# Transposes of three late steps moved from TensorE to the DMA queue, and two leftover steps placed one step later

## The chip, the cores and the metric

The kernel runs on one core of one Trainium2 chip. The metric is the time in device microseconds of one execution. It is given as the median of several runs, and beside it stands one profiled execution, whose trace gives the durations used here. The engines are called as in the profile: PE (TensorE matmul), PEld (its weight load), DVE (VectorE), ACT (ScalarE), POOL (GpSimd) and SP (SyncE, which here only issues DMAs).

## What is computed

Eight batches, eight heads, 576 positions, head size 64. A retention layer (causal attention with a decay per head and no softmax) is followed by a gated unit whose gate is a causal convolution of five taps.

```python
scores = scale * np.matmul(q, k.transpose(0, 1, 3, 2))
gamma = 1.0 - 2.0 ** (-5.0 - np.arange(H, dtype=np.float32))
Dmat = np.where(rel >= 0, gamma[:, None, None] ** rel[None, :, :], 0.0)
x = np.matmul(scores * Dmat, v)          # then heads side by side: (8, 576, 512)
...
for k in range(5):
    gate_pre += conv_w[k][None, None, :] * xp[:, k:k + S, :]
gate = 1.0 / (1.0 + np.exp(-gate_pre))
out = gate * (x @ w_val) @ w_out
```

## The kernel before

**Steps.** The batches are worked in four pairs, numbered u = 0 to 3, with bb = 0 or 1 for the batch in the pair. The 576 positions of a batch are cut into two chunks of 256 (n = 0, 1) and 64 leftover positions. A *full step* treats one chunk of one batch, all eight heads. A *leftover step* treats the 64 leftover positions of both batches of a pair at once. That makes 16 full steps and 4 leftover steps, numbered 0 to 19. `REMD` says how many places after its pair's last full step a leftover step is put into the list. With `[2, 0, 2, 0]` the leftover steps are 6, 9, 16 and 19. Step 17 is the first chunk of the last batch, step 18 its second chunk, step 19 the last leftover step.

**One step.** `load` (L90 to L107) issues the DMAs of k, q and v on the SP queue: three of 512 KB for a full step, six of 128 KB for a leftover step. `cast` (L223) multiplies k and q by the decay factors on POOL and turns k, q and v into bf16 tiles `kb`, `qb`, `vb` (L236, L243). `transp` (L246) transposes `kb` and `qb` on PE against an identity, eight 128x128 blocks each for a full step and four for a leftover step (L256), and copies the results out of PSUM to `kt` on ACT and `qt` on DVE (L264, L266 in the helper `copy`). `state` and `state_sum` (L307, L325, L327) carry the sum over earlier chunks forward. `scores` (L283) multiplies `kt` and `qt`, DVE puts the mask on (L290, tile `am`), `inter` (L345) adds the part of earlier chunks, `values` (L358) multiplies by `vb`, and `evac` copies the result to the tile `xt` of the pair, or `xr` for leftovers.

**Blocks of the gated unit.** When the result of a batch is complete, `push_block` puts its work into a list: two convolutions (`conv`, L442, gate on ACT at L448), four value products (`val`, L537, with the product by the gate on DVE at L539, tile `zt`) and output products (`outp`, L544, copied by ACT at L547 to `ob` and stored by SP at L575). For a block near the end (number 8) half of the convolution runs as taps on ACT, POOL and DVE (L462 to L468), and for the last three blocks as products and taps (L478 to L502).

**What sets the order.** The schedule is written out by hand: instructions go to each engine in the program's order. Lists of short codes (`FULL`, `PART`, `LASTS`) give the order inside a step; a number such as `4.45` calls `fill`, which takes block work from the list until its cost is used up. In step s the loads of step s + 4 are issued first, then the casts of step s + 2; the transposes of step s + 1 come at the code `T`. After step 19 the codes of `TAIL` give the rest, where `w` takes the next item of the list. The SP queue holds loads and stores in one order; each DMA there uses one of eight semaphores in turn and is issued after the DMA eight places before it has landed.

Of the kernel before, what the change touches and what calls it, by code (L numbers as in the profile page):

```python
# [15 lines left out]
BF16 = mybir.dt.bfloat16  # L16
# [15 lines left out]
def kernel(  # L32
# [10 lines left out]
    nc = tc.nc  # L43
# [3 lines left out]
    P = 128  # L47
# [4 lines left out]
    HP = H // 2  # L52
# [7 lines left out]
    TPS, DSS, CAP = False, False, 2.0  # L60
    PB, EV, TE = [4, 2, 2], "DA", "AD"
    C1, LO = "PPP", "1vo23"
    PATH, TAIL, LASTS = {9: {2: 'D', 3: 'A'}, 11: {2: 'D', 3: 'A'}, 10: {0: 'D', 1: 'A', 2: 'D', 3: 'A'}}, ['w', 'w', 't9.201234', 'w', 'p10.301234', 's10.30', 't10.001234', 's10.31', 'w', 'w', 'w', 'w', 'c9.0', 't10.201234', 'w', 'p11.301', 'w', 'p11.323', 'w', 'p11.34', 's11.30', 'w', 's11.31', 'c11.0', 'v9.0', 'v9.1', 'v9.2', 'v9.3', 't11.201234', 'o9.0', 'o9.1', 'v11.0', 'v11.1', 'v11.2', 'v11.3', 'o11.0', 'o11.1', 'v10.0', 'v10.1', 'v10.2', 'v10.3', 'z10'], [['Sa', '4.5', 'I', 'Sb', 'Q5', 'G5', 'T', '7.15', 'Vb', 'p9.301234', 'Va', 's9.30', 's9.31', 'E', 'B'], ['1.8', 'I', 'Sr', 'p10.101234', '6.65', 'Vr', 's10.10', 'E', 'B', 's10.11']]
    SPL, REMD = 0, [2, 0, 2, 0]
    VC = "P"
    PULL = [2, 3]
    LATE = True
# [4 lines left out]
    at = ctx.enter_context(tc.tile_pool(name="at", bufs=3))  # L72
# [19 lines left out]
    NS = len(steps)  # L92
    st = {}

    def load(s):
        u, bb, n = steps[s]
        r = st.setdefault(s, {})
        R = 1 if bb is None else 2
        for nm, src in (("kf", k), ("qf", q), ("vf", v)):
            t = ld.tile([P, H, R, D], F32, tag=f"{nm}{R}", name=nm, bufs=2 if bb is None else 4)  # L100
            if bb is None:
                for x in range(2):
                    nc.sync.dma_start(out=t[x * HF:(x + 1) * HF, :, 0, :],
                                      in_=src[2 * u + x, :, NSC * SC:S, :].rearrange("h p d -> p h d"))
            elif s > 0:
                nc.sync.dma_start(
                    out=t.rearrange("p h r d -> p h (r d)"),  # L107
                    in_=src[2 * u + bb, :, n * SC:(n + 1) * SC, :].rearrange("h (p r) d -> p h (r d)", r=R))
            r[nm] = t
        if s == 0:  # L110

            for hv in range(2):
                hs = slice(hv * HP, (hv + 1) * HP)
                for nm, src in (("kf", k), ("qf", q), ("vf", v)):
                    nc.sync.dma_start(
                        out=r[nm][:, hs].rearrange("p h r d -> p h (r d)"),
                        in_=src[0, hs, 0:SC, :].rearrange("h (p r) d -> p h (r d)", r=2))
# [105 lines left out]
    def cast(s):  # L223
        u, bb, n = steps[s]
        r = st[s]
        R = 1 if bb is None else 2
        shp = [P, R, H, D]
        f0 = n * 2
        nb = 2 if bb is None else 4
        kb = cs.tile(shp, BF16, tag=f"kb{R}", name="kb", bufs=nb)  # L230
        qb = cs.tile(shp, BF16, tag=f"qb{R}", name="qb", bufs=nb)
        vb = cs.tile(shp, BF16, tag=f"vb{R}", name="vb", bufs=nb)

        how = C1 if s == 1 else "PP" + VC[s % len(VC)]
        for e, dst, src, f in ((how[0], kb, r["kf"], fk), (how[1], qb, r["qf"], fq)):
            (nc.vector if e == "D" else nc.gpsimd).tensor_tensor(  # L236
                dst, src.rearrange("p h r d -> p r h d"),
                f[:, f0:f0 + R, :].unsqueeze(3).to_broadcast(shp), op=ALU.mult)
        vsrc = r["vf"].rearrange("p h r d -> p r h d")
        if how[2] == "A":  # L240
            nc.scalar.copy(vb, vsrc)
        else:
            nc.gpsimd.tensor_copy(vb, vsrc)  # L243
        r.update(qb=qb, kb=kb, vb=vb)

    def transp(s, which="kq"):  # L246
        if s >= NS:
            return
        r = st[s]
        R = 1 if steps[s][1] is None else 2  # L250
        for nm in which:
            src = r[nm + "b"]
            tp = (scp if TPS else glp).tile([P, HP, R, P], BF16, tag="sc" if TPS else "gps", name="tp" + nm)
            for hp in range(HP):
                for rr in range(R):
                    nc.tensor.transpose(tp[:, hp, rr, :],  # L256
                                        src[:, rr, 2 * hp:2 * hp + 2, :].rearrange("p a d -> p (a d)"), ident)
            t = at.tile([P, HP, R, P], BF16, tag=f"{nm}t{R}", name=nm + "t", bufs=1 + R)
            copy(TE[nm == "q"], t, tp)
            r[nm + "t"] = t  # L260

    def copy(engine, dst, src):
        if engine == "A":
            nc.scalar.copy(dst, src)  # L264
        else:
            nc.vector.tensor_copy(dst, src)  # L266
# [121 lines left out]
    work = []  # L388
# [285 lines left out]
    def explicit(op):  # L674

        if op == "w":
            f, a, cost = work.pop(0)
            f(a)
            return
        b, _, a = op[1:].partition(".")  # L680
        f = blocks[int(b)][op[0]]
        if op[0] == "z":
            f()
        elif op[0] in "pt":
            f(int(a[0]), [int(x) for x in a[1:]])
        elif op[0] == "s":
            f(int(a[0]), int(a[1]))
        else:
            f(int(a))

    LOOK = 4
# [29 lines left out]
    for s in range(NS):  # L721
        u, bb, n = steps[s]
        last = u == B // 2 - 1
        if s + LOOK < NS:
            load(s + LOOK)
        if s > 1 and s + 2 < NS:
            cast(s + 2)
        for op in (PART if bb is None else FIRST if s == 0 else SECOND if s == 1 else FULL[n]) if s < NS - len(LASTS) \
                else LASTS[s - NS]:
            if op[0] in "cvopstgz":  # L730
                explicit(op)
            elif op[:2] in ("D0", "D2"):
                prep_diag(int(op[1]), nc.vector if op[3] == "D" else nc.gpsimd)
            elif s == 0 and ":" in op:

                first(op[0], "ab".index(op[1]), op[3:])
                if op[:2] == "Eb":
                    usable.append("conv2")
            elif op == "Sa":
                scores(s, GA)  # L740
            elif op == "Sb":
                scores(s, GB)
            elif op == "Sr":
                scores(s, ALL)
            elif op == "I":
                inter(s)
            elif op == "T":
                transp(s + 1)
            elif op in ("Tk", "Tq"):
                transp(s + 1, op[1])  # L750
            elif op == "C1":
                cast(1)
            elif op == "C2":
                cast(2)
            elif op[0] == "Q":
                pull(3, int(op[1]))
            elif op[0] == "G":
                pull(2, int(op[1]))
            elif op == "C3":
                cast(3)  # L760
            elif op == "WV":
                prep_wval()
                usable.append("val")
            elif op == "WO":
                prep_wout()
                usable.append("outp")
            elif op == "Va":
                values(s, GA)
            elif op == "Vb":
                values(s, GB)  # L770
            elif op == "Vr":
                values(s, ALL)
            elif op == "X":
                state(s + 1)
            elif op == "XS":
                state_sum(s + 1, 0)
                state_sum(s + 1, 1)
            elif op == "E":
                evac(s)
            elif op == "B":  # L780
                b = 2 * u + (bb or 0)
                if bb is None:
                    if u % 2 == 1:
                        push_block(xrs[u // 2], None, 0, [(b - 2 + j, NSC * SC, REM) for j in range(4)])
                elif (last and bb == 1) or b <= SPL:
                    push_block(xts[u], bb, n * SC, [(b, n * SC, SC)])
                elif n == NSC - 1:
                    push_block(xts[u], bb, 0, [(b, 0, NSC * SC)])
            else:
                fill(float(op))  # L790
    tail[0] = 0
    work.extend(late)
    for op in TAIL:
        explicit(op)
    assert not work and not any(pend.values())


# [28 lines left out]
```

## Time and profile before

| | us |
|---|---|
| median of 5 runs | 182.36 |
| lowest, highest | 181.17, 183.59 |
| the profiled execution | 183.08 |
| its span in the trace | 181.0 |

| engine | busy us | share of the span |
|---|---|---|
| PE | 156.5 | 86% |
| DVE | 125.3 | 69% |
| POOL | 109.5 | 61% |
| ACT | 105.2 | 58% |

The span is the time from the first to the last instruction in the trace; the execution's own time is 2.1 us longer. The page cuts the span into 40 equal slices of about 4.5 us and gives the busy share of each in tenths. The chain that ended last is followed back from the last instruction: at each step to what released it, or to the instruction before it on its engine. In a group's row the numbers after the bar are busy time, mean duration in ns, and the idle time of the engine before these instructions with what ended it. In rows of the timeline or the chain the first number is the start in us from the span's start, the second the duration. The granted TensorE clock is full in all slices.

### The profile page before, as it was taken

The numbers are of one execution on the slowest core, as the hardware profiler recorded it, in microseconds if no ns is written. First come the engines' busy times: TensorE is split into PE (matmuls) and PEld (weight loads), VectorE is DVE, ScalarE is ACT, GpSimd is POOL, SyncE is SP. The second block draws the span as 40 slices with busy tenths as digits, with TensorE's granted clock in tenths as the row PEclk, the third lists the DMA queues.
The fourth block names the chain that finished last, engine by engine and source line by source line (L and its number), as shares of the span: only waits on it lengthen the run. The fifth ranks groups of instructions, "written<-read, shape, count | busy, mean of one in ns | idle before, by whom it ended". The sixth has DMA issues, their size and how long they took to land.

```text
span 181.0 us, 7614 instructions
## 1 busy us (share of the span) xinstructions
PE 156.5 (86%) x3289; PEld 104.7 (58%) x3313; DVE 125.3 (69%) x240; ACT 105.2 (58%) x216; POOL 109.5 (61%) x105
## 2 busy tenths in 40 slices
PE   0479779967999998899999999698999889999991
PEld 0347557746666666566676587375669534447560
DVE  2968673569669645967479759646859897964931
ACT  6653775545561756257347655533678958689451
POOL 5059389977547957298836992497414697274300
PEclk9999999999999999999999999999999999999999
DMA  5999999999899989999998999997533003205334
GB/s 153 292 295 380 308 266 279 298 295 263 247 287 283 197 223 344 323 272 298 331 297 224 302 207 307 257 299 201 123 118 123 0 0 120 116 4 231 116 81 156
DMA packets 69183, 40.35 MB, mean 223 GB/s; under 512 B 14218, under 2 KB 63646, under 8 KB 69150
## 3 DMA queue, kind: packets, MB, share of 16 engines
q1 hardware_dynamic: 69120, 39.85, 78.5%
q8 instruction: 26, 0.43, 1.0%
q14 instruction: 7, 0.06, 0.1%
q10 hardware_dynamic: 30, 0.01, 0.0%
HBM read 30.42 MB, written 9.44 MB: 220 GB/s over the span
## 4 chain that ended last, share of the span: by engine, by line
PE 68%; DVE 13%; ACT 8%; issue 4%; DMA 3%; SPq 1%; DVEq 0%; ACTq 0%
PE ops L544 16%; PE cps L442 16%; PE vps L537 12%; DVE am L290 5%; PE o L358 4%; PE tpk L256 4%; PE sc L283 4%; PE tpq L256 4%; ACT gt L448 3%; DMA vf<-in_v_dram 3%; DVE accs L468 3%; PE o L345 3%; PE ds L307 2%; DVE sn L325 2%; DVE zt L539 2%
## 5 line engine op out<-in xcount | busy, mean ns | idle before, releaser
L236 POOL TENSOR_TENSOR kb<-kf,fk 128x1024 bf16<-128x1024 f32 (+1 forms) x19 | 32.7, 1723 | 35.9 <-DMA kf<-in_k_dram 35.8
L290 DVE TENSOR_TENSOR am<-sc,mask_c 128x512 bf16<-128x512 f32 x64 | 40.9, 681 | 4.1 <-PE sc L283 4.1
L442 PE MATMUL cps<-xt,diag 64*64 64x512 bf16 (+1 forms) x640 | 35.5, 353 | 3.0 <-issue 1.6
L236 POOL TENSOR_TENSOR qb<-qf,fq 128x1024 bf16<-128x1024 f32 (+1 forms) x19 | 32.7, 1723 | 1.6 <-DMA qf<-in_q_dram 1.0
L544 PE MATMUL ops<-wout,zt 128*128 128x512 bf16 x122 | 31.7, 380 | 1.4 <-issue 0.3
L442 PEld LDWEIGHTS <-diag 64*64 64x64 bf16 x760 | 25.3, 109 | 12.8 <-issue 4.9
L539 DVE TENSOR_TENSOR zt<-gt,vps 128x256 bf16<-128x256 f32 (+1 forms) x48 | 25.0, 549 | 9.8 <-PE vps L537 5.3
L537 PE MATMUL vps<-xt,wval 128*128 128x512 bf16 (+1 forms) x150 | 29.8, 334 | 1.9 <-ACT xt L264 0.9
L448 ACT ACTIVATE gt<-cps 128x512 f32<-128x512 f32 (+1 forms) x38 | 17.2, 505 | 22.2 <-PE cps L442 22.2
L537 PEld LDWEIGHTS <-wval 128*128 128x128 bf16 x192 | 17.7, 97 | 13.7 <-issue 1.9
L547 ACT COPY ob<-ops 128x512 f32<-128x512 f32 x34 | 19.6, 584 | 9.6 <-PE ops L544 7.4
L264 ACT COPY kt<-tpk 128x1024 bf16<-128x1024 bf16 (+1 forms) x19 | 17.5, 923 | 9.1 <-PE tpk L256 8.9
L243 POOL CAST vb<-vf 128x1024 bf16<-128x1024 f32 (+1 forms) x19 | 18.0, 948 | 5.1 <-DMA vf<-in_v_dram 4.4
L264 ACT CAST xt<-o 128x512 bf16<-128x512 f32 (+1 forms) x17 | 12.3, 722 | 14.4 <-PE o L358 11.7
L544 PEld LDWEIGHTS <-zt 128*128 128x128 bf16 x136 | 12.0, 98 | 14.5 <-DVE zt L539 2.3
L283 PE MATMUL sc<-qt,kt 64*64 64x128 bf16 (+1 forms) x576 | 18.4, 221 | 0.8 <-DVE am L290 0.8
L266 DVE CAST xt<-o 128x512 bf16<-128x512 f32 (+1 forms) x17 | 12.2, 717 | 9.5 <-PE sc L283 5.9
L327 ACT CAST w<-sn 128x256 bf16<-128x256 f32 x30 | 12.0, 405 | 9.7 <-DVE sn L323 6.0
L266 DVE COPY qt<-tpq 128x1024 bf16<-128x1024 bf16 (+1 forms) x19 | 11.9, 627 | 6.6 <-PE tpq L256 6.5
L325 DVE TENSOR_TENSOR sn<-ds,sn 128x256 f32<-128x256 f32 x23 | 9.8, 425 | 9.6 <-PE ds L307 6.3
L358 PEld LDWEIGHTS <-vb 64*64 64x64 bf16 x544 | 10.0, 106 | 7.9 <-issue 7.4
L358 PE MATMUL o<-am,vb 64*64 64x128 bf16 (+1 forms) x544 | 12.4, 216 | 2.3 <-DVE am L290 2.2
(90 smaller groups left out, 197.3 us busy)
## 6 DMA issues: line engine op xcount, KB each, us to landing
out_dram<-ob SPq DMA_DIRECT2D x31, 256.0 KB, 4.3
kf<-in_k_dram SPq DMA_DIRECT2D x15, 512.0 KB, 6.9
qf<-in_q_dram SPq DMA_DIRECT2D x15, 512.0 KB, 7.5
vf<-in_v_dram SPq DMA_DIRECT2D x15, 512.0 KB, 7.6
out_dram<-ob SPq DMA_DIRECT2D x10, 128.0 KB, 2.8
wvf<-in_moe_w_val_dram SPq DMA_DIRECT2D x2, 512.0 KB, 6.9
wof<-in_moe_w_out_dram SPq DMA_DIRECT2D x2, 512.0 KB, 7.9
kf<-in_k_dram SPq DMA_DIRECT2D x8, 128.0 KB, 5.0
```

Of the source, the lines that this page charges most:

```text
L236: (nc.vector if e == "D" else nc.gpsimd).tensor_tensor(dst, src.rearrange("p h r d -> p r h d"), f[:, f0:f0 + R, :].unsqueeze(3).to_broadc ...
L264: nc.scalar.copy(dst, src)
L266: nc.vector.tensor_copy(dst, src)
L283: nc.tensor.matmul(sc[hh][HS[x], a, rj, :].rearrange("p (r i) -> p r i", r=R), lhsT=r["kt"][HS[hh], hp, rj, HS[x]], rhs=r["qt"][HS[hh], hp ...
L290: nc.vector.tensor_tensor(am, sc[hh], mk.rearrange("p j i x -> p j (i x)").unsqueeze(1).to_broadcast(shp), op=ALU.mult)
L358: nc.tensor.matmul(o[x][HS[hh], hp, :], lhsT=r["vb"][HS[x], rj, 2 * hp + hh, :], rhs=r[("am", hps[0], hh)][HS[x], a, rj, :], start=(a == 0 ...
L442: nc.tensor.matmul(fold(cps[i][HS[r ^ i]]), lhsT=diag[HS[r], p2, kk, d0 + i, :], rhs=win(d0 + i, kk)[HS[r]], start=(kk == 0 and p2 == 0), ...
L448: nc.scalar.activation(gt, cps[i], AF.Sigmoid)
L537: nc.tensor.matmul(fold(vp), lhsT=wval[:, do, d, :], rhs=win(do, PAD), start=(do == 0), stop=(do == DT - 1))
L539: nc.vector.tensor_tensor(z[0][:, d, 0:N], g[d], vp, op=ALU.mult)
L544: nc.tensor.matmul(op, lhsT=z[0][:, d, m * P:(m + 1) * P], rhs=wout[:, d, :], start=(d == 0), stop=(d == DT - 1))
L547: nc.scalar.copy(ob, op)
```

## The change

Two settings and the code for them:

- `DTS = [17, 18, 19]`: for these three steps `transp` does nothing. Instead `cast` issues, right after the three casts, two DMA transposes on the SP queue, from `kb` to `kt` and from `qb` to `qt` (256 KB each for steps 17 and 18, 128 KB each for step 19). A DMA transpose waits on SP for the cast that writes its source. In the steps where this happens (15, 16 and 17) the loads of step s + 4 are issued after these casts and transposes instead of ahead of them. Only step 15 has such loads: those of step 19.
- `REMD = [3, 1, 2, 0]`: the leftover steps of the first two pairs become steps 7 and 10 instead of 6 and 9. The list is then: step 6 first chunk of batch 3, step 7 leftovers of pair 0, step 8 second chunk of batch 3, step 9 first chunk of batch 4, step 10 leftovers of pair 1; from step 11 on nothing moves.
- The tail's `w` codes are evened out with the number of items left in the list, so that another order still ends with an empty list.

On each engine, the order of instructions differs from before in steps 5 to 10 and by the instructions removed in steps 16 to 18; the SP queue also has the six transposes. In that queue the order from the last four stores ahead of step 19's loads is: two transposes of step 17, six loads of step 19, two transposes of step 18, two stores, two transposes of step 19, then the remaining stores.

```diff
+    DTS = [17, 18, 19]
...
-    SPL, REMD = 0, [2, 0, 2, 0]
+    SPL, REMD = 0, [3, 1, 2, 0]
...
         r.update(qb=qb, kb=kb, vb=vb)
+        if s in DTS:
+
+            for nm in ("k", "q"):
+                t = at.tile([P, R, HP, P], BF16, tag=f"{nm}t{R}", name=nm + "t", bufs=1 + R)
+                nc.sync.dma_start_transpose(out=t.rearrange("p r a i -> p (r a) i"),
+                                            in_=r[nm + "b"].rearrange("p r h d -> p (r h d)"))
+                r[nm + "t"] = t.rearrange("p r a i -> p a r i")
 
     def transp(s, which="kq"):
-        if s >= NS:
+        if s >= NS or s in DTS:
             return
...
-            f, a, cost = work.pop(0)
-            f(a)
+            if work:
+                f, a, cost = work.pop(0)
+                f(a)
...
-        if s + LOOK < NS:
+        if s + LOOK < NS and s + 2 not in DTS:
             load(s + LOOK)
         if s > 1 and s + 2 < NS:
             cast(s + 2)
+        if s + LOOK < NS and s + 2 in DTS:
+            load(s + LOOK)
...
-    for op in TAIL:
-        explicit(op)
+
+    ahead = TAIL.count("w") - len(work)
+    for op in ["w"] * -ahead + TAIL:
+        if op == "w" and ahead > 0:
+            ahead -= 1
+        else:
+            explicit(op)
```

## The prediction

> **What bounds the kernel now.** I read the page first: the busy tenths of the engines and of the DMA, and the chain that ended last.
>
> ```profile
> PE   0479779967999998899999999698999889999991
> ...
> DMA  5999999999899989999998999997533003205334
> ...
> PE 68%; DVE 13%; ACT 8%; issue 4%; DMA 3%; SPq 1%; DVEq 0%; ACTq 0%
> ...
> L264 ACT COPY kt<-tpk 128x1024 bf16<-128x1024 bf16 (+1 forms) x19 | 17.5, 923 | 9.1 <-PE tpk L256 8.9
> ...
> L266 DVE COPY qt<-tpq 128x1024 bf16<-128x1024 bf16 (+1 forms) x19 | 11.9, 627 | 6.6 <-PE tpq L256 6.5
> ```
>
> PE carries 68% of the chain and is nearly full in most slices. The DMA engines are full until about slice 28 (127 us), yet hold 3% of the chain: loads run ahead of PE. After 127 us they are almost idle. The last two rows are the evacuations that follow each transpose pair (L256): 923 ns on ACT, 627 ns on DVE.
>
> Next, the chain of waits between 124 and 152 us, where the three steps lie whose transposes go.
>
> ```profile
> 128.68 0.45 PE tpk L256 x8
> 129.12 0.45 PE tpq L256 x8
> ...
> 132.15 0.23 PE sc L283 x16
> 132.37 0.55 PE tpk L256 x8
> 132.93 0.45 PE tpq L256 x8
> 133.37 0.22 PE ops L544
> ...
> 135.54 0.42 DVE sn L325
> ...
> 146.70 0.09 DVE qt L266
> 146.78 0.17 issue
> 146.95 1.27 DVE zt L539 x2
> ```
>
> Two transpose pairs, those for steps 17 and 18, stand on the chain: PE does nothing else there. From 135.5 us DVE leads (sums, masks L290, conv taps L468). The third pair, for step 19, ran on PE at 142.96 us while DVE led; only its copy `qt` shows on the chain, 0.09 us and 0.17 us of issue.
>
> Then the SP queue, POOL, and one PE row, from the timeline.
>
> ```profile
> 118.67 4.74 SPq L575 DMA_DIRECT2D out_dram<-ob  x4
> 123.46 1.37 SPq L103 DMA_DIRECT2D kf<-in_k_dram  x2
> ...
> 126.90 1.32 SPq L103 DMA_DIRECT2D vf<-in_v_dram  x2
> ```
> ```profile
> 117.34 1.90 POOL L236 TENSOR_TENSOR qb<-qf,fq 128x1024 bf16<-128x1024 f32 x1
> ...
> 122.41 1.90 POOL L236 TENSOR_TENSOR qb<-qf,fq 128x1024 bf16<-128x1024 f32 x1
> ```
> ```profile
> 138.36 0.22 PE L283 MATMUL sc<-qt,kt 64*64 64x128 bf16 x1
> ```
>
> SP issues the last stores until 123.4 and the loads of step 19 from 123.46 to 128.2. The casts that feed the new transposes end at 119.2 (step 17) and 124.3 (step 18), before SP comes to them. First uses: the scores at 132.15 (step 17) and 138.36 (step 18).
>
> Last, the DMA view of two stretches: 56.4 to 64.9 us, where 256-byte pieces dominate, and 123.4 to 132.2, where the queue empties.
>
> ```profile
> DMA packets 4954, 1.72 MB, mean 203 GB/s; under 512 B 3201, under 2 KB 4951, under 8 KB 4951
> ```
> ```profile
> out_dram<-ob SPq DMA_DIRECT2D x1, 256.0 KB, 2.0
> out_dram<-ob SPq DMA_DIRECT2D x1, 128.0 KB, 2.6
> ```
>
> **The change, part by part.**
>
> *Removed: three transpose pairs.* On PE 16, 16 and 8 matmuls; on the chain 0.45 + 0.45 = 0.90 us (step 17) and 0.55 + 0.45 = 1.00 us (step 18). The pair of step 19 lies beside DVE work: nothing on PE. The three ACT copies of `kt` (1.01, 1.01, 0.59 us) are off the chain: nothing. Of the DVE copies of `qt` (0.69, 0.68, 0.41 us) the first two lie in stretches where DVE waits for PE (1.30 us before `xr` at 132.26, 1.04 before `sn` at 135.52); the third gives its 0.26 us. Before the step-16 masks DVE has 1.28 us of `zt` work, which would let those masks move only 0.74 us, but their values wait behind an output product of 1.8 us, so PE keeps its 0.90. Sum: 0.90 + 1.00 + 0.26 = 2.16, say 2.2 us, if the transposed tiles are there in time.
>
> *Added: six DMA transposes on the SP queue*, four of 256 KB and two of 128 KB. The trace of before has none. With T the time that one of 256 KB holds the DMA engines (or SP, if that is longer):
> - The last store ahead landed at 125.4 (issued 122.8, 2.6 us). `qt` of step 17 lands at 125.4 + 2T + 1.0; the 1.0 is my estimate of a landing's tail, from the 2.0 us that a 256 KB store took on an empty queue less 256 KB at 290 GB/s (0.9 us). It is wanted at 132.15 - 0.90, say 131.2. Spare while T is under 2.4.
> - Behind those two stand the six loads of step 19: 768 KB at 203 GB/s, 3.9 us. `qt` of step 18 lands at 125.4 + 2T + 3.9 + 2T + 1.0 = 130.3 + 4T. It is wanted at 138.36 - 1.90 = 136.5. Spare while T is under 1.55.
> - Step 19 wants its pair at about 147; that pair waits for a cast that ends near 134. Hidden, and it costs nothing unless T is over 8 or so.
>
> T from both sides: 256 KB at 289 GB/s, the rate of 512-byte loads (80 to 100 us), gives 0.9; at the 203 GB/s of 256-byte pieces, 1.3. [...] I take 1.3, since the source rows of a block are 256 bytes, the size in that row. Then `qt` lands at 129.0 (2.2 us early) and at 135.5 (1.0 us early): the transposes cost nothing. What hides them is PE's work of steps 15 to 17.
>
> [...]
>
> *Moved past on the queues.* The loads of step 19 now stand behind two transposes and arrive 2T = 2.6 us later; its cast on POOL ends near 135.5 instead of 132.9. The next POOL work (`accs` adds at 138.23, 136.3 after the shift) still finds POOL free; if not, it has until the gate at 158.7. The stores behind the transposes wait for the step-19 cast: at most 4 us, and output buffers are next wanted at 150.97. Nothing. The load of step 19 is issued after the step-17 cast instead of before; POOL's order is unchanged there.
>
> *Moved: the leftover steps of the first two pairs*, from 6 and 9 to 7 and 10, with their six loads and POOL casts. On PE the six steps 5 to 10 (52.8 to 91.2 us) do the same instructions in another order; from step 11 on the order is that of before. PE is idle for 1.6 of these 38.4 us, 0.94 of it at 72.93, where a value product waits for ACT's `xt`. In the new order that product follows a leftover step, which writes `xr`, so that wait goes; but the first convolution (now inside step 7) follows a step that writes the same `xt`, and its evacuation takes ACT 0.77 us: about 0.7 comes back. The 512 KB loads come up 768 KB earlier (about 2.7 us at 290 GB/s) and their step 6 us earlier. The state product of the moved step is due near 55.0, and its casts end near 51 by the same spacing as before. For step 8 they end at 62.9, due near 65. Bounds: -1.0 (all waits but 0.6 go) to +1.5 (both stay, and a load is 0.6 late); I take 0.
>
> *The end*: the tail's list comes out in the same order on every engine. Nothing.
>
> **Sum.** The profiled execution took 183.08 us (span 181.0 and 2.1 around it): 183.08 - 2.2 = 180.9. It stood 0.72 above the median of 182.36, so on the median: 180.2 us. A measurement of this kernel can tell about 1% (1.8 us) from no change.
>
> **Rivals.**
> 1. *The transposes land late.* Place: the scores of steps 17 and 18, on PE's one queue. For: no row shows a DMA transpose; the spare is only 1.0 us. Against: the DMA engines are idle after 128. From T = 1.55 it costs 4 x (T - 1.55); at T = 2.1 the gain is gone; at 2.6 the time is 182.36 - 2.2 + 4.2 = 184.4, over 1% slower. At T = 5 `qt` of step 17 is 5.2 us late and that of step 18 another 8.6: 194. [...]
> 2. *The removed transposes covered waits.* PE arrives sooner and waits for DVE's `zt` and masks. For: DVE leads from 135.5. Against: the waits of 1.30 and 1.04 us of DVE on PE in that stretch. If only one pair counts: 182.36 - 0.9 = 181.4.
> 3. *The moved steps stall.* The casts of steps 6 or 8 come late, spare 4 and 2 us. For: POOL waits for `kf` in most steps, up to 5.5 us. Against: the load order is the same in bytes from step 8 on. At +1.5: 181.7; from a stall of 2.2 us no gain is left.
>
> **How the numbers follow.** Hidden and neutral, 180.2 (own range 179.2 to 181.1): 0.48. Late by a little (T 1.55 to 2.6; 180.2 to 184.4): 0.10. Late by much: 0.20, since my price is a guess across kinds of transfer. Covered waits, 181.4: 0.10. Stall in the middle, about 181.7: 0.12. Faster by over 1% (under 180.5): 0.40 of the first, 0.02 each of the little-late and the stall: 0.44. Slower by over 1% (over 184.2): all of the much-late, 0.02 of the little-late, 0.04 of the stall: 0.26. Within 1%: 0.30. The range of 179.0 to 185.5 leaves out some 0.03 below and 0.17 of the much-late above.
>
> **What would show it.** Right: no `tpk` after about 124 us; PE from the step-17 scores on about 0.9, and from the step-18 state on 1.9 us earlier against the end of step 15; DMA transposes near 1.3 us apart; POOL idle before `accs`. Wrong: PE waiting for a DMA at L283 or L345 in steps 17 or 18 (rival 1), SP issue rows of several us for a transpose (rival 1, through SP), DVE waits ahead of the step-17 products (rival 2), PE idle over 1.6 us in steps 5 to 10, with POOL `kb` waits ahead of it (rival 3).

## The result, and the profile after

| | changed kernel | the kernel before, same chip | ratio, 95% interval |
|---|---|---|---|
| first measurement, median us (runs) | 181.62 (28) | 182.38 (54) | 0.9853 (0.9814 to 0.9893) |
| second measurement, with the last experiments | 181.02 (12) | 181.40 (28) | 0.9958 (0.9915 to 1.0002) |
| profiled execution, us | 180.26 | 183.08 | |
| its span, us | 178.6 | 181.0 | |

The medians are over all runs, the ratios over the runs within 1.5% of the kernel's fastest alone; in the first measurement these are 6 of 29, because one run took 177.74 us, so its ratio of 0.9853 cannot be read as the gain. The forecast was 180.2 us, 2.2 under the median of before. The medians gained 0.76 and 0.38 us. The means over all runs lie 0.80 us apart in the first measurement, with a 95% interval of 0.1 to 1.5, and 0.12 us in the second, with an interval from 1.1 faster to 0.9 slower. A gain is shown in the first and not in the second, and in both it is smaller than forecast. Lines of the changed kernel are numbered 8 higher than before around the steps.

First the same rows of the page as before: busy tenths of PE and of the DMA engines, the DMA queues, the chain, and the row of the scores.

```profile
PE   0479779967999999999999989898996949999990
...
DMA  4999999999989999989999999999899302406343
...
q1 hardware_dynamic: 74432, 41.17, 86.6%
q8 instruction: 25, 0.41, 1.0%
...
PE 64%; DVE 10%; ACT 8%; DMA 7%; issue 5%; SPq 2%; POOL 1%; DVEq 0%; ACTq 0%; POOLq 0%
...
L291 PE MATMUL sc<-qt,kt 64*64 64x128 bf16 (+1 forms) x576 | 17.9, 221 | 2.1 <-DMA qt<-qb 1.7
```

DMA rose from 3% to 7% of the chain, and the scores wait 1.7 us for a DMA-written `qt`. The PE tenths show the place: a 6 in the slice from 134.0 to 138.4 us, where before had only 8 and 9; the 4 lies later, from 142.9 to 147.3, where DVE's taps lead. The chain through both is next (start, duration, what):

```profile
131.51 5.00 DMA qt<-qb
136.50 0.14 issue
136.64 0.42 PE sc L291 x16
137.06 2.16 PE cps L450 x39
...
140.51 0.68 DVE am L298
141.19 1.73 DVE accs L476
142.95 1.64 DVE accs L476
144.59 0.09 DVE zt L547
```

The DMA transpose of step 18's q is issued at 131.51 and has landed at 136.50; PE takes up the scores 0.14 us later. Before the change the chain had two transpose pairs on PE and no DMA here. The SP queue of the changed kernel shows how the transposes go out:

```profile
121.73 2.57 SPq L250 DMA_TRANSPOSE kt<-kb  x1
124.41 1.25 SPq L250 DMA_TRANSPOSE qt<-qb  x1
125.71 1.39 SPq L104 DMA_DIRECT2D kf<-in_k_dram  x2
127.14 1.50 SPq L104 DMA_DIRECT2D qf<-in_q_dram  x2
128.69 1.31 SPq L104 DMA_DIRECT2D vf<-in_v_dram  x2
130.11 1.28 SPq L250 DMA_TRANSPOSE kt<-kb  x1
131.51 1.34 SPq L250 DMA_TRANSPOSE qt<-qb  x1
...
134.05 2.09 SPq L250 DMA_TRANSPOSE kt<-kb  x1
136.23 1.22 SPq L250 DMA_TRANSPOSE qt<-qb  x1
```

Each transpose holds SP for 1.2 to 2.6 us, and between the two pairs stand the six loads of step 19 (4.3 us of issue). The pair of step 18 goes out at 130.11 and 131.51.

**Where the time went.** Between fixed instructions of DVE, the same in all kernels, I measured stretches of each trace. "Steps 5 to 11" runs from 54.9 to 95.3 us of before; "transposes" from 128.2 to the state sum of step 18 (135.5), where the two pairs stood; "masks and taps" from there to the gate product at 146.95. "Pauses" are PE's waits marked `issue` (no releaser in the profile) from 20 to 131 us, good to 0.1 us.

| kernel | steps 5 to 11 | transposes | masks and taps | pauses |
|---|---|---|---|---|
| before | 40.40 | 7.32 | 11.43 | 2.4 |
| changed | 38.82 | 5.54 | 12.68 | 3.4 |
| changed, second profile | 39.16 | 6.35 | 12.55 | 1.6 |
| transposes only | 40.38 | 5.53 | 12.10 | 1.1 |
| move only | 38.98 | 7.31 | 11.43 | 4.2 |
| changed, step 19's loads last (two) | 39.04, 38.83 | 5.53, 5.53 | 10.37, 11.14 | 3.4, 3.1 |
| changed, step 18 on PE | 39.74 | 6.43 | 11.10 | 6.5 |
| unmoved, step 19's loads last (two) | 40.52, 40.39 | 5.53, 5.54 | 11.36, 10.68 | 1.8, 0.5 |
| unmoved, step 18 on PE | 40.38 | 6.43 | 11.10 | 0.8 |
| unmoved, transposes added for nothing | 40.39 | 7.32 | 11.43 | 1.3 |
| unmoved, no q loads | 40.40 | 7.32 | 11.42 | 0.4 |
| moved, no q loads | 39.06 | 7.31 | 11.44 | 1.1 |

Three readings: the transposes save 1.8 us where they stood (1.0 in the second profile); the changed kernel loses 1.25 us of that in the next stretch (1.1 in the second profile, which is left with 0.1 lost over both); and the move saves 1.2 to 1.6 us in steps 5 to 11 in every profile but one (0.7, where a pause of 0.6 falls into them), while the pauses grow.

My theory after this: the transposes are worth what was forecast, but the pair of step 18 lands too late behind the loads of step 19; and the move's saving is given back by PE waiting for its own instructions. The rivals: the removed transposes had covered waits; or the move is simply worth nothing.

### The profile page after: what moved, and what is told of

Its sections match the earlier page's. It is cut to its first block, busy times and chain, and to the rows that moved or that the text cites. A ratio compares the mean times of both kernels' runs of the same rounds, so it can differ in the third digit from the quotient of the medians.

```text
span 178.6 us, 7549 instructions
## 1 busy us (share of the span) xinstructions
PE 152.2 (85%) x3252; PEld 101.8 (57%) x3273; DVE 124.2 (70%) x237; ACT 103.2 (58%) x213; POOL 109.8 (62%) x105
## 4 chain that ended last, share of the span: by engine, by line
PE 64%; DVE 10%; ACT 8%; DMA 7%; issue 5%; SPq 2%; POOL 1%; DVEq 0%; ACTq 0%; POOLq 0%
PE cps L450 18%; PE ops L552 15%; PE vps L545 10%; PE sc L291 4%; DVE am L298 4%; PE o L366 4%; PE tpk L264 4%; PE o L353 3%; DMA qt<-qb 3%; DMA vf<-in_v_dram 3%; PE tpq L264 3%; DMA kf<-in_k_dram 2%; ACT kt L272 2%; DVE accs L476 2%; PE ds L315 2%
## 5 line engine op out<-in xcount | busy, mean ns | idle before, releaser
L450 PE MATMUL cps<-xt,diag 64*64 64x512 bf16 (+1 forms) x640 | 35.0, 353 | 2.2 <-ACT xt L272 1.2
L450 PEld LDWEIGHTS <-diag 64*64 64x64 bf16 x760 | 26.2, 109 | 10.9 <-issue 3.6
L291 PE MATMUL sc<-qt,kt 64*64 64x128 bf16 (+1 forms) x576 | 17.9, 221 | 2.1 <-DMA qt<-qb 1.7
L272 ACT COPY kt<-tpk 128x1024 bf16<-128x1024 bf16 (+1 forms) x16 | 14.9, 931 | 3.1 <-PE tpk L264 2.9
L274 DVE COPY qt<-tpq 128x1024 bf16<-128x1024 bf16 (+1 forms) x16 | 10.1, 633 | 8.0 <-PE tpq L264 8.0
L291 PEld LDWEIGHTS <-kt 64*64 64x64 bf16 x576 | 12.8, 109 | 2.8 <-issue 2.8
```

The lines of the kernel that those rows point to most:

```text
L291: nc.tensor.matmul(sc[hh][HS[x], a, rj, :].rearrange("p (r i) -> p r i", r=R), lhsT=r["kt"][HS[hh], hp, rj, HS[x]], rhs=r["qt"][HS[hh], hp ...
L450: nc.tensor.matmul(fold(cps[i][HS[r ^ i]]), lhsT=diag[HS[r], p2, kk, d0 + i, :], rhs=win(d0 + i, kk)[HS[r]], start=(kk == 0 and p2 == 0), ...
```

## The experiments

The edits are against the changed kernel unless the text says otherwise. Medians are of all runs, with the kernel before on the same chip in brackets.

**One part alone.**

```diff
-    SPL, REMD = 0, [3, 1, 2, 0]
+    SPL, REMD = 0, [2, 0, 2, 0]
```

> The leftover steps stay at 6 and 9; the three steps' transposes are DMAs. Theory 1 (the prediction's sum: transposes -2.2 us, move 0): ratio to before 0.988. Theory 2 (the two traces: the move gave 1.3 us by step 11, the transposes 1.8 us on PE by the state product of step 18, of which a wait for the last transposed tile gives back about 1 us and more): ratio 0.993 to 0.996, with the same wait of 1 to 2 us at the scores of step 18.

181.66 us (182.49), ratio 0.9924 (0.9885 to 0.9964), nearer theory 2 than theory 1. The stretch of the transposes is 1.79 us shorter, as in the changed kernel; PE waits 1.1 us for `qt` of step 18, and masks and taps take 0.67 us more than before. In this profile 1.5 us more went at the end, where the granted PE clock was 0.65 and 0.78 from 146 to 152 us; it is 1.00 there in both profiles of the changed kernel, so those 1.5 us are not put down to the change.

```diff
-    DTS = [17, 18, 19]
+    DTS = []
```

> All transposes on PE; the leftover steps at 7 and 10. Theory 1: ratio to before 1.000, PE idle in steps 5 to 10 about 1.5 us as before. Theory 2: ratio 0.993, those six steps about 1.3 us shorter.

182.69 us (182.49), ratio 1.0007 (0.9973 to 1.0041). In the total the move is worth something between 0.5 us gained and 0.7 lost, although steps 5 to 11 take 1.42 us less: the total is that of theory 1, the stretch that of theory 2.

**The order of the loads, and fewer transposes.** The loads of step 19 go behind the transposes of step 18 instead of ahead of them:

```diff
-        if s + LOOK < NS and s + 2 in DTS:
-            load(s + LOOK)
+        if s == 16:
+            load(19)
```

> As the changed kernel, but the six loads of step 19 are issued behind the transposes of step 18 instead of ahead of them. Theory 2: the wait at the scores of step 18 goes, the DVE taps meet less of POOL's adds, ratio to before 0.976 to 0.982 (0.5 to 1.6 us under the changed kernel). Rival (DVE leads there anyway, so the wait costs nothing): the ratio stays at 0.985. Second rival: step 19's cast comes some 4 us later and POOL's adds behind it are late for the gate: 0.985 or worse, with a wait for POOL on the chain.

182.14 us (182.49; six runs from 178.63 to 185.27, no ratio). The total does not bear out the forecast. The profile, its shortest run, does: no wait for a DMA at the scores, and masks and taps 2.31 us shorter than in the changed kernel. Step 18 left on PE:

```diff
-    DTS = [17, 18, 19]
+    DTS = [17, 19]
```

> As the changed kernel, but step 18's pair is transposed on PE again. Theory 1 (each pair on the chain is worth its own PE time): 1.0 us slower than the changed kernel, ratio 0.990. Theory 2 (the late landing of step 18's pair gives back at least as much as that pair saved): same as the changed kernel, 0.983 to 0.987, and no wait for a DMA at the scores of step 18.

180.89 us (182.49), ratio 0.9906 (0.9873 to 0.9939). One pair in place of two saves 0.89 us in the stretch of the transposes; there is no wait behind it. Its profiled execution was a long one, 185.17 us with 6.5 of pauses, so only the two stretches are read from it. The ratio is the 0.990 of theory 1, but both forecasts were set against the 0.9853 of the changed kernel, which its second measurement did not repeat, so the total does not decide between them; the missing wait is as theory 2 had it.

**The disputed cost by itself.** To the kernel before I added four DMA transposes of 256 KB and one of 128 KB whose result nobody reads, on an otherwise idle queue at step 19:

```diff
+        if s == 19:
+            for i, tag in enumerate(("kf2", "qf2", "vf2", "kf2", "qf2")):
+                c = 1 if i == 4 else 2
+                scr = ld.tile([P, 4 * c, P], BF16, tag=tag, name="scr", bufs=4)
+                nc.sync.dma_start_transpose(out=scr, in_=kb18[:, 0:c].rearrange("p r h d -> p (r h d)"))
```

> The kernel before, with five DMA transposes added whose results nobody reads: four of 256 KB and one of 128 KB, back to back on the SP queue at the start of step 19, where the DMA engines are idle (after about 136 us). The prediction's price: each lands 1.3 us after the one before, the first about 2.3 us after its issue. The trace of the changed kernel (step 18's pair landed 4.1 and 4.9 us after issue, with step 19's loads ahead): if those loads alone made them late, the first lands here within 2.5 us; if a transpose has a long way of its own, it takes 3.5 us or more. Time as before.

A single run, 180.74 us. The SP queue's row, the tile's own answer, and the busy tenths of the DMA engines from 133 to 148 us (0.375 us a digit):

```profile
134.21 9.11 SPq L734 DMA_TRANSPOSE scr<-kb  x5
```

```profile
L734 SPq DMA_TRANSPOSE scr<-kb x5: 1280/1321/2536, 134.2 to 142.0; - x5
...
DMA to landing us min/median/max: 2.6/3.9/4.6
```

```profile
DMA  0097691001999999000599999997920000000000
```

SP is held 1.28 to 2.54 us by each, 9.11 us for the five. In the trace they land at 141.37, 142.69, 143.98 and 144.61 from the second on (the first has no record): 1.3 us apart for 256 KB and 0.63 for 128 KB. So the pace of 1.3 that the forecast took is right, and the delay is not: 3.9 us in the median from issue to landing, with no load of step 19 near. The DMA row shows part of it: the first of the transposes' 256-byte packets starts at 136.68, 2.5 us after the first issue, and from 138.9 to 140.1 almost none starts, though three transposes have been issued. Why is open.

**Both cures without the move.** The old `REMD` with all three transposes and the loads last, and the old `REMD` with step 18 on PE:

```diff
-    SPL, REMD = 0, [3, 1, 2, 0]
+    SPL, REMD = 0, [2, 0, 2, 0]
...
-        if s + LOOK < NS and s + 2 in DTS:
-            load(s + LOOK)
+        if s == 16:
+            load(19)
```

> Leftover steps at 6 and 9, DMA transposes for the three steps, step 19's loads behind step 18's transposes. If the wait at the scores of step 18 costs: under the run with transposes only (0.9924) by 0.5 to 1.5 us, ratio 0.984 to 0.990. If not: 0.992. No wait for instructions between 44 and 51 us, as in the two earlier kernels with unmoved steps.

179.72 us (181.72), ratio 0.9915 (0.9878 to 0.9952). The ratio is the 0.992 that was expected if the late landing costs nothing; the medians say more (2.00 us under before, where transposes only was 0.83 under), so the totals leave this open.

```diff
-    DTS = [17, 18, 19]
-    SPL, REMD = 0, [3, 1, 2, 0]
+    DTS = [17, 19]
+    SPL, REMD = 0, [2, 0, 2, 0]
```

> Leftover steps at 6 and 9, DMA transposes for steps 17 and 19 alone. The stage sums (0.9 us from step 17, 0.3 from step 19, nothing given back): ratio 0.993, as much as with all three pairs. If the move of the leftover steps helps by itself: slower than the moved kernel of the same pairs (0.9906).

180.41 us (181.72), ratio 0.9938 (0.9903 to 0.9973), near the 0.993 expected. Beside these two, the third kernel of this group was once more the changed one with step 19's loads last, with the diff shown above:

> The changed kernel with step 19's loads behind step 18's transposes, as in an earlier run whose one profile was 1.7 us shorter than the changed kernel's but whose other times were not. If the profile speaks for all runs: ratio 0.976 to 0.982. If what it gains is lost in PE's waits for instructions, which differ from run to run: a median within 0.5 us of the changed kernel's 181.6.

180.24 us (181.72), ratio 0.9912 (0.9876 to 0.9949). Neither forecast came (0.976 to 0.982, or within 0.5 us of 181.6). With the loads last the moved and the unmoved order are the same, 0.9912 and 0.9915: again nothing for the move.

**Where the move's saving goes.** The pauses on PE look like this. In the move-only kernel's chain, and then in that of before:

```profile
95.06 0.17 PE tpq L264 x3
95.23 1.94 issue
97.16 0.45 PE tpq L264 x5
```

```profile
115.45 0.70 PE cps L442 x11
116.15 1.65 issue
117.79 1.76 PE cps L442 x29
```

PE stops in the middle of a group of equal matmuls, with nothing left to wait for. Numbered in PE's own order, instructions where it stops are 1468, 1724, 2234, 3761, 4270, 4524, 4779 and 5035: 256 apart, or a multiple of it but for a few records missing from the traces. The queue called `instruction` (q8) moves 25 or 26 packets of 16,384 bytes in an execution. In before one of these runs from 115.27 for 1.05 us, and PE resumes 1.47 us after its end. In the fourteen traces 48 waits of PE marked `issue` last 0.2 us and more; 47 end 1.2 to 1.7 us after the end of such a packet (the other, of 0.22 us, follows a long one). So these pauses look like waits for instructions. Of the six unmoved kernels with full loads the sums are 0.5 to 2.4 us (mean 1.3), of the six moved ones 1.6 to 6.5 (mean 3.7, and 3.1 without the long profile).

That is enough to take back the saving. Up to the value product at which the stretch of the transposes begins, the six unmoved kernels took 126.5 us in the mean, with 1.2 us of pauses; the five moved ones without the long profile took 126.6, with 3.0. Without the pauses that is 125.3 against 123.6. Part of them, up to 1.7 us in a kernel, lies between 44 and 51 us, where PE's own order is still the old one: it first differs at 52.6 us. What differs by then, ahead of the steps 5 to 10 named with the change, is SP's order, from 40.3 us on, and that of POOL's casts, from 45.0.

If a full DMA queue makes these packets late, less load traffic must let the move pay. The q loads of all full steps but the first were left out of both orders, and q taken from k's tile, so these two kernels compute something else:

```diff
+            if nm == "qf" and bb is not None and s > 0:
+                r["qf"] = r["kf"]
+                continue
```

> The kernel before, with the q loads of all full steps but the first left out (q is taken from k's tile, so the result is not the reference's): 512 KB less in each of these steps, so that the DMA queue is no longer full. It is the partner of the next kernel, which differs only in the move. Theory (PE's pauses without a releaser, at instructions about 256 apart, come from small fetches that wait behind a full DMA queue): in steps 11 to 16 and before step 5 their sum falls to under 0.5 us (0.5 to 2.15 in the five unmoved profiles so far), and the span to about 179. Rival (the pauses have nothing to do with DMA traffic): they stay as they are, 0.5 to 2 us, at the same instructions.

180.54 us (181.40), ratio to before 0.9969 (0.9941 to 0.9998).

> The move alone (no DMA transposes), with the same q loads left out as in the kernel above. The move by itself shortened steps 5 to 10 by 1.4 us in every profile, and its time came out at 1.0007 of before. Theory (the 1.4 us are given back by PE's pauses, which only a full DMA queue makes): with the traffic gone nothing is given back, so this kernel is about 1.4 us under its unmoved partner, a ratio near 0.992 between the two, and the pauses of steps 11 to 16 are under 0.5 us in both. Rival (the order itself gives it back, or the 1.4 us were waits for loads that are gone here too): the two take the same time within 0.5 us.

179.11 us (181.40), ratio to before 0.9887 (0.9838 to 0.9936). Between the two medians lie 1.43 us, between the means 1.55 with a 95% interval of 0.7 to 2.4. PE's waits marked `issue`, first without the move, then with it (sum, times, longest):

```profile
PE cps L445 <- issue: 0.4, 1, 0.4
```

```profile
PE cps L453 <- issue: 1.2, 2, 1.0
PE o L369 <- issue: 0.9, 1, 0.9
```

And the move alone with full loads:

```profile
PE tpq L264 <- issue: 1.9, 1, 1.9
PE o L366 <- issue: 1.3, 1, 1.3
PE o L353 <- issue: 0.7, 2, 0.4
```

In the unmoved kernel 0.4 us is left, as the theory wanted. In the moved one steps 11 to 16 are clean, but one pause of 0.9 us at 45 us stays (the 1.2 of L453 lies nearly all ahead of 20 us), so the theory was too bold there. That profile, of the longest of its six runs, still has 1.5 us more of pauses ahead of the transposes than its partner. The total is as the theory said: the move pays 1.4 us when the loads are thin, and the rival (no difference) falls. So the totals show that the giving back needs the load traffic. That it works through the instruction packets is read from the traces and was not tried by itself, and why the moved order meets them more often is open; its loads stand in another order, but that too was not tried alone.

**Side by side.** The changed kernel again, and on the same chip the unmoved kernel with step 19's loads last:

> The changed kernel itself once more, beside the next kernel on the same chip. Theory and rival alike: 181 to 182 us, steps 16 to 19 up to the last masks' product 0.5 us shorter than before (18.2 of 18.75), and a wait of PE for the DMA transpose of step 18 of 1 to 2 us at the scores.

181.02 us (181.40), ratio 0.9958 (0.9915 to 1.0002).

> All three DMA transposes, the loads of step 19 behind the transposes of step 18, and the leftover steps where the kernel before has them; a second measurement, now side by side with the changed kernel. Theory (of the changed kernel's gain in steps 16 to 19 about 1.3 us is lost to the late transpose of step 18 and to the collision of DVE's taps with POOL's adds, and the move brings nothing in sum): 1.0 to 1.5 us under the changed kernel, near 180 us, with no wait for DMA at the scores of step 18. Rival (what the order of loads saves is made up elsewhere, and the move is worth what it saves in steps 5 to 10): the same as the changed kernel within 0.5 us, or above it.

180.55 us (181.40), ratio 0.9930 (0.9890 to 0.9970). It is 0.47 us under the changed kernel by the medians and 1.0 by the means, with an interval from 2.2 under to 0.2 over: the total does not settle it. The profiles do for the place: masks and taps take 10.68 us against 12.55, and 10.37 to 11.36 in the four profiles with the loads last against 12.55 and 12.68 in the changed kernel's two. The unmoved kernel's SP queue, then its DVE:

```profile
121.60 1.45 SPq L250 DMA_TRANSPOSE kt<-kb  x1
123.16 1.82 SPq L250 DMA_TRANSPOSE qt<-qb  x1
125.09 1.26 SPq L250 DMA_TRANSPOSE kt<-kb  x1
126.45 2.38 SPq L250 DMA_TRANSPOSE qt<-qb  x1
128.88 1.38 SPq L104 DMA_DIRECT2D kf<-in_k_dram  x2
```

```profile
138.35 1.29 DVE L298 TENSOR_TENSOR am<-sc,mask_c 128x512 bf16<-128x512 f32 x2 [0.50 <-PE sc L291]
139.56 2.90 DVE L476 SCALAR_TENSOR_TENSOR accs<-xt,cw,accs 128x512 f32<-128x512 bf16 x2
```

The pair of step 18 goes out 5 us earlier and has landed by 130.7, well ahead of the scores.

In the changed kernel's second profile the pair of step 17 was late as well, by 0.59 us. That is most of the 0.81 by which its stretch of the transposes exceeds the first profile's. Transposes, masks and taps together take 18.9 us there, against the 18.2 that were expected and the 18.75 of before:

```profile
129.09 0.42 PE L291 MATMUL sc<-qt,kt 64*64 64x128 bf16 x16 [0.59 <-DMA qt<-qb]
136.47 0.42 PE L291 MATMUL sc<-qt,kt 64*64 64x128 bf16 x16 [1.61 <-DMA qt<-qb]
```

## Why the prediction was right and wrong

**Removed transposes: right.** Forecast 0.90 + 1.00 us on PE; measured 1.78 in the stretch, with PE's last `tpk` at 121.9. The copy of `qt` for step 19 was put at 0.26; without it masks and taps take 11.10 us in place of 11.43 where nothing else changes there (both kernels with step 18 on PE), 0.33. Together 2.11 of 2.16. The rival of covered waits falls: a removed pair gave its 0.9 in every kernel except where the next tile came late, in the changed kernel's second profile.

**The DMA transposes cost nothing: wrong, and this is the step that failed.** It said that `qt` of step 18 lands at 130.3 + 4T, 1.0 us early. Put on the changed kernel's clock, which by the end of the last stores ahead (121.6 instead of 123.4) runs 1.8 us earlier, it was to land at 133.7 and to be wanted at 134.7. PE came at 134.9; the tile landed at 136.5, 2.8 us later than forecast. The time of the pair's turn came out: 125.4 + 2T + 3.9 = 131.9, on the changed clock 130.1, and SP issued it at 130.11. That is luck. The forecast counted 6.5 us from the last store's landing (123.6 on the changed clock); SP began the first transposes at 121.73, 1.9 us before that, and took 8.4 us to issue them and the six loads. The pace of 1.3 was right, as the added transposes show, but T was also to cover SP where SP is slower, and the four held it 6.4 us, 1.6 each; by the formula 4 x (T - 1.55) that is worth 0.2 us. Mis-sized was the end: 2T + 1.0 = 3.6 us from the pair's start to the second landing, and measured 6.4. With the loads behind it, where it follows the pair of step 17 directly, the pair still needs 5.6 to 5.7 us (four profiles): about 2 us of the miss stay without the loads. The tail of 1.0 us came from a plain store; in the changed kernel's two profiles the transposes of 256 KB landed 4.1 to 5.4 us after their issue began. Step 17 was no safer: forecast 2.2 us early, its `qt` came 0.59 us late in the second profile. The "late by a little" rival had the right place and the wrong cause: it asked for T over 1.55.

The "late by much" rival falls: it asked for a T over 2.6, and nothing in the changed kernel or among the added transposes came to that. The added ones of 256 KB, eight 128x128 blocks each, landed 1.3 us apart and held SP for at most 2.54 us; in the changed kernel the longest hold was 2.57 us.

**What the wait cost, which no step had.** Of the 1.7 us that PE waits, DVE passes only 0.53 on to its masks. But the convolution behind the scores, ACT's products and POOL's adds come the whole 1.7 us later: POOL's adds start 7.55 us after the state sum in before and 9.26 in the changed kernel. So they now start together with DVE's taps. Changed kernel, DVE and POOL, then before, DVE and POOL:

```profile
139.91 1.29 DVE L298 TENSOR_TENSOR am<-sc,mask_c 128x512 bf16<-128x512 f32 x2 [1.03 <-PE sc L291]
141.11 3.48 DVE L476 SCALAR_TENSOR_TENSOR accs<-xt,cw,accs 128x512 f32<-128x512 bf16 x2
```

```profile
134.54 3.43 POOL L472 TENSOR_TENSOR accs<-accs,prod 128x512 f32<-128x512 f32 x2 [0.48 <-ACT prod L470]
141.09 2.95 POOL L472 TENSOR_TENSOR accs<-accs,prod 128x512 f32<-128x512 f32 x2 [3.12 <-ACT prod L470]
```

```profile
143.06 1.29 DVE L290 TENSOR_TENSOR am<-sc,mask_c 128x512 bf16<-128x512 f32 x2 [0.50 <-PE sc L283]
144.27 2.43 DVE L468 SCALAR_TENSOR_TENSOR accs<-xt,cw,accs 128x512 f32<-128x512 bf16 x2
```

```profile
143.07 3.08 POOL L464 TENSOR_TENSOR accs<-accs,prod 128x512 f32<-128x512 f32 x2 [1.41 <-ACT prod L462]
```

Two taps take 3.48 us in place of 2.43. The sum of the stretches: -1.78 (transposes) - 0.33 (copy) + 0.53 (wait) + 1.05 (taps) = -0.53, and the table gives the same (18.22 against 18.75). With the loads last the same sum is between -1.9 and -2.9 in four profiles.

**Moved past on the queues: right.** POOL's casts of step 19 ended at 134.06, and the adds then waited 0.48 us for ACT, not for the casts. With the loads last the casts end between 135 and 138, and that costs nothing either: in the two profiles where POOL's adds fall behind the first pair of taps, that pair takes 1.54 us and not 2.43.

**The move at nothing: right in the total, by cancellation, which is luck.** The 0.94 us wait of the value product went, as said, and steps 5 to 11 gained about 1.4, beyond the bound of -1.0. The forecast did not see the pauses that take it back; the stall by late loads (rival 3) did not come.

**The tail: right.** Its 34.03 us before are 34.04 after.

So the forecast of 180.2 had a saving of 2.2 us with nothing against it, where the first profile has 0.53 in the stretches that carry it and the second none. That the profiled span fell by 2.4 us all the same, close to the forecast, is luck: the move's 1.58 in steps 5 to 11 and 0.48 ahead of step 5 make up the rest, with 0.13 lost between. Those last parts change from one execution to the next.

## What to carry to other kernels

Price a DMA transpose in three parts: the time it holds the issuing queue, the pace, and the delay until it has landed; here they were 1.2 to 2.6, 1.3 and 2.4 to 5.4 us. A transfer that is needed soon goes ahead of loads that are needed late: here moving one line took away a wait of 1.7 us in the profiles, though the totals do not settle what that is worth. And when a stretch gets shorter in every profile but the total does not, look for waits without a releaser elsewhere before calling the stretch a gain.

## What of the hardware was not expected

**DVE beside POOL.** In the profiles of before and of the changed kernel one tap (two fp32 or bf16 inputs from SBUF) takes 0.75 us by itself and 1.64 to 1.80 when it meets a POOL add that has just begun; a POOL add takes 1.27 us alone and 1.60 to 1.75 when it begins beside a tap under way. They seem to take turns: in the changed kernel POOL's adds end at 142.37 and 144.04, and the taps beside them 0.55 us later each; the tap ended at 142.92, and the add beside it 1.12 later.

**PE and its instructions.** The queue q8 moved 25 packets of 16,384 bytes in the changed kernel and 26 in before; PE has 6,525 records (matmuls and weight loads) in the one and 6,602 in the other. That is 261 and 254 records to a packet, close to the 256 that lie between the places of the pauses. A pause takes up to 1.9 us (2.2 in the long profile), at other places in each execution. Their sums differ by 1.8 us between the two profiles of the changed kernel; whether they make the spread of its runs (177.7 to 184.0 us) was not tried.
